# The first two chunks times the first weight pair in float32: a fused attention and MLP kernel on one core

## The chip, the cores and the metric

The kernel runs on one core of a Trainium2 chip. The metric is the device time of one execution in microseconds (us). Engines are called by the profile's names: PE is TensorE (PEld its weight loads), DVE is VectorE, ACT is ScalarE, POOL is GpSimd, and SP is SyncE, which here only starts transfers.

## The reference

A decaying linear attention (4 batches, 8 heads, 768 tokens, 64 per head) is followed by a two-layer perceptron with a leaky ReLU over 3072 tokens, 512 wide, with 2048 hidden units. The inputs of the attention are float32, the weights are float64, and the output is float32.

```python
for b in range(nb):                                   # blocks of 64 tokens
    intra = einsum('bhic,bhjc->bhij', qb, kb) * Dmask # Dmask: lam ** (i - j), lower triangle
    intra = einsum('bhij,bhjd->bhid', intra, vb)
    inter = einsum('bhid,bhde->bhie', qb * lam_pow, kv_state)
    out[:, :, sl] = intra + inter
    kv_state = lam_block * kv_state + einsum('bhsd,bhse->bhde', kb * rev_pow, vb)
x = out.transpose(0, 2, 1, 3).reshape(B * S, H * D)   # 3072 x 512
h = x @ w_in                                          # 512 -> 2048
g = maximum(0.01 * h, h)
y = g @ w_out                                         # 2048 -> 512
```

## The kernel before

**Chunks and groups.** The 3072 tokens are 24 chunks of 128, six per batch. Four chunks make a group of 512 tokens, so there are six groups (0 to 5). The weights w_in are cut into eight pairs of 128 hidden units (0 to 7).

**Attention of a chunk.** `load_kq` and `load_v` fetch keys, queries and values. `transposes` (L391) turns keys and queries on PE, ACT copies them out of PSUM (L402, L403), and keys and queries are scaled by powers of lam (L407 and L411; `KM` and `QS` say up to which chunk DVE may or must do that, after which POOL does). `scores` makes scores and state products in the PSUM tile `psc` (PE, L312; chunks below `GOFIRST` do the scores first), DVE scales the scores (L440) and adds the states (L445, L447), and POOL decays the states (L450). `outputs` makes the chunk's outputs in `po`, in three steps of PE; between the second and third a copy of two columns (L479) reads `po`.

**Three-way split.** PE multiplies in float32r[...]. So tokens and weights are each split into a high part, a low part and a difference: xh, xl, xm (L495 on ACT, L496 and L498 on DVE) and wh, wl, wm (L581 or L579, L584, L590). A product is then three float32r products, high with high, low with low and difference with difference, summed in one PSUM bank; the sum is rescaled by ACT (L646) between the second and the third.

**Weights.** `w_in(p)` (stage "wi") fetches two halves of float64 weights into a raw buffer (issued by ACT, L554), rebuilds float32 values in the tile `w32` (ACT L566, L568, L570; DVE L572, L573), and splits them in `parts`, which ends with `difference`. `w32` holds one pair at a time.

**First layer.** `up(g, p, lo, hi)` multiplies the chunks lo to hi of group g with pair p (L628: each of the three products has four matmuls per half of the pair), applies the leaky ReLU (ACT, L649) into one of two tiles `gs`, and stores the result to the DRAM tile `G` (SP, L652). The PSUM banks b10, b11 and b2 are used in turn. L265 makes transposes of an identity that nobody reads; `busy` puts them where PE is expected to idle. From group 2 on the work is regular. Then the second layer (`down_load`, `down`, L688) reads `G` back and multiplies with the split w_out.

**What sets the order.** A list `seq`, written out by hand for the start, names stages: "a" a whole chunk's attention, "b" the start of the pipelined form, "r" a pipelined round, "wi" a pair of weights, "up" a product. Each stage adds operations with a planned length and their data dependencies to `Plan`; `emit` then places one operation after another on the engine where it can begin first by the planned lengths, ties going to the lower rank (the place in `seq` plus a given addition). This fixes the order of each engine; at run time each engine follows its own order and waits on semaphores. In `up` the planned lengths of the four matmuls of a product are 0.91, 0.7, 0.49 and 0.29 us for 4, 3, 2 and 1 chunks (512, 384, 256 and 128 columns).

Of the kernel before, what the change touches and what calls it, by code (L numbers as in the profile page):

```python
# [8 lines left out]
F32 = mybir.dt.float32  # L9
# [153 lines left out]
def kernel(  # L163
# [21 lines left out]
    NG = NCH // GC  # L185
    T = GC * C
    WARM = 9
    LATER = 2.0
    KT, EARLY = "b11", 0
    QS = 4  # L190
    KM = 2
    NRAW = 3
    TURN = 3
    SLACK, GSLACK = 4.0, 2.0
    EARLY_SLACK = 1.0
    GOFIRST = 3
    SUBL, FIRST = 0.75, -8.0

    DV = 12
# [9 lines left out]
    def sb(shape, name, dt=F32):  # L209
        return pool.tile(shape, dt, name=name, tag=name)  # L210
# [16 lines left out]
    w32f = w32.rearrange("p h n -> p (h n)")  # L227
    tt = [raw[-1][:, i * T:(i + 1) * T] for i in range(2)]
    gs = [sb([P, 2, T], f"gs{i}") for i in range(2)]
    WO = [dram.tile([P, 2 * d_model], F32, name=f"wo{p}", tag=f"wo{p}") for p in range(NP)]  # L230
    G = [[dram.tile([P, 2 * T], F32, name=f"g{g}_{p}", tag=f"g{g}_{p}") for p in range(NP)] for g in range(NG)]

# [222 lines left out]
    def outputs(c, between=lambda: None):  # L455
        b, n, i = of(c)
        tv, qsT = kqv[2][i], qsTs[i]

        def own():
            for y in range(HP):  # L460
                for hi in range(2):
                    for t in range(2):
                        h = 2 * y + hi
                        a, z = place(h)
                        quad(po[:, t, y, :], t, tv[:, h, :], sc[:, a, z, :], hi, start=y == 0)

        def inter(m):
            for y in range(HP):
                t = y % 2 ^ m
                for hi in range(2):  # L470
                    if n or t:
                        a, z = place(2 * y + hi)
                        quad(po[:, t, y, :], a, state[(2 * c + t - 1) % 4][:, z, :], qsT[:, z, tokens(t)], hi)

        needs = [f"qsT{i}", f"st{2 * c % 4}"] + ([f"st{(2 * c - 1) % 4}"] if n else [])
        add("PE", 0.61, own, ["sc", f"v{i}"], ["po"])
        add("PE", 0.24, lambda: inter(0), needs, ["po"])

        add(("DVE", "ACT"), (0.15, 0.25), lambda e: (nc.vector.tensor_copy if e == "DVE" else nc.scalar.copy)(seen_po, po[:, :, 0, 0]),  # L479
            ["po"], ["seen_po"], rank=-3.0)  # L480
        between()
        add("PE", 0.46, lambda: inter(1), needs + ["seen_po"], ["po"])


        g, cc = c // GC, c % GC
        xh, xl, xm = (x[:, :, cc * C:(cc + 1) * C] for x in X[g % 2])
        y = po[:, :, lower, :]

        def tok(z):
            return z.rearrange("p k (t i) -> p t k i", t=2)  # L490

        h, l, m = (f"x{z}{g % 2}{cc}" for z in "hlm")

        def uses():
            add("ACT", 0.6, lambda: nc.scalar.activation(out=tok(xh), in_=y, func=AF.Copy, bias=0.0, scale=NEAR), ["po"], [h])  # L495
            add("DVE", 0.7, lambda: nc.vector.tensor_tensor(tok(xl), y, tok(xh.bitcast(F32)), op=ALU.subtract),  # L496
                ["po", h], [l])
            add("DVE", 0.7, lambda: nc.vector.scalar_tensor_tensor(xm, xl.bitcast(F32), -S, xh.bitcast(F32), op0=ALU.mult, op1=ALU.add),  # L498
                [h, l], [m], rank=LATER if c < GC else 0.0)

        return uses
# [73 lines left out]
    def parts(p, src, keys):  # L575
        wh, wl, wm = W[p]
        def head(e):
            if e == "ACT":
                nc.scalar.activation(out=wh, in_=src, func=AF.Copy, bias=0.0, scale=NEAR / S)  # L579
            else:  # L580
                nc.vector.tensor_scalar(wh, src, NEAR / S, None, op0=ALU.mult)  # L581

        add(("ACT", "DVE"), (1.05, 0.7), head, keys, [f"wh{p}"])
        add("DVE", 1.25, lambda: nc.vector.scalar_tensor_tensor(wl, wh.bitcast(F32), -S, src, op0=ALU.mult, op1=ALU.add),  # L584
            keys + [f"wh{p}"], [f"wl{p}"])
        difference(p)

    def difference(p):
        wh, wl, wm = W[p]
# [3 lines left out]
    def w_in(p):  # L593
        for h in range(2):
            to_float32("wi", p, h, w32[:, h, :], f"w32{h}")
        parts(p, w32f, ["w320", "w321"])

    ATT = ["fk", "fq", "sc"] + [f"{x}{i}" for x in ("k", "q", "v", "kT", "qT", "qsT") for i in range(2)] + [f"st{i}" for i in range(4)]
    NR = 4
# [7 lines left out]
    def w_out_parts(p):  # L607
        j = p % NR
        add("DMA", 1.5, lambda: nc.sync.dma_start(out=graw[j], in_=WO[p]), [f"WO{p}"], [f"gr{j}"], rank=-3.0)
        parts(p, graw[j], [f"gr{j}"])  # L610


    n_t = n_g = 0
    n_b = -EARLY

    def up(g, p, lo=0, hi=GC):


        nonlocal n_g, n_b
        x, w = X[g % 2], W[p]  # L620
        jg, n_g = n_g % 2, n_g + 1
        toks = slice(lo * C, hi * C)
        n = (hi - lo) * C
        us = {4: 0.91, 3: 0.7, 2: 0.49, 1: 0.29}[hi - lo]

        def product(dst, f, z, start=False):
            for kk in range(KO):
                nc.tensor.matmul(dst, lhsT=w[z][:, kk * 2 * P + f * P:kk * 2 * P + (f + 1) * P], rhs=x[z][:, kk, toks],  # L628
                                 start=start and kk == 0, stop=kk == KO - 1, skip_group_check=True)

        def keys(z):
            return [f"w{z}{p}"] + [f"x{z}{g % 2}{cc}" for cc in range(lo, hi)]


        blocks = [[0, 1]] if 2 * n <= T else [[0], [1]]
        y = gs[jg].rearrange("p f t -> p (f t)")[:, :2 * n].rearrange("p (f t) -> p f t", f=2)
        for fs in blocks:
            kb = ("b10", "b2")[n_b % 2] if n_b < 0 else ("b10", "b11", "b2")[n_b % 3]
            n_b += 1
            b = bank[kb][:, :len(fs) * n].rearrange("p (f t) -> p f t", f=len(fs))  # L640
            r = y[:, fs[0]:fs[-1] + 1, :]
            for i, f in enumerate(fs):
                add("PE", us, lambda f=f, d=b[:, i, :], first=i == 0: product(d, f, 0, first), keys("h"), [kb])
                add("PE", us, lambda f=f, d=b[:, i, :]: product(d, f, 1), keys("l"), [kb])
            ns = 0.6 if len(fs) * n == T else 0.4
            add("ACT", ns, lambda b=b: nc.scalar.activation(out=b, in_=b, func=AF.Copy, bias=0.0, scale=S + 1.0), [], [kb], rank=-1.5)  # L646
            for i, f in enumerate(fs):
                add("PE", us, lambda f=f, d=b[:, i, :]: product(d, f, 2), keys("m"), [kb])
            add("ACT", ns, lambda b=b, r=r: nc.scalar.activation(out=r, in_=b, func=AF.Prelu, bias=0.0, scale=1.0 / WS, alpha=0.01),  # L649
                [kb], [f"gs{jg}"], rank=-1.5)  # L650
        move(1.5 * (hi - lo) / GC + 0.1,
            lambda: nc.sync.dma_start(out=G[g][p].rearrange("p (f t) -> p f t", f=2)[:, :, toks], in_=y), [f"gs{jg}"], [f"G{g}{p}"], slack=GSLACK)  # L652

# [22 lines left out]
    def down(g, p):  # L676

        nonlocal n_t
        for tb in range(GC):
# [43 lines left out]

    seq = [("a", 0), ("a", 1), ("a", 2), ("a", 3), ("wi", 1), ("b", 4), ("r", 4), ("up", 0, 1), ("wi", 0), ("r", 5),
# [4 lines left out]
    nxt, n_out, begin = 3 * GC, 0, len(seq)  # L731
    steps = [(g, p) for g in range(2, NG) for p in range(NP)]
    for n, (g, p) in enumerate(steps):
# [12 lines left out]
    for g in range(NG):  # L746
        for p in range(0, NP, 2):
            seq += [("dl", g, p), ("dl", g, p + 1), ("dn", g, p)]

    freed = False  # L750
    for n, x in enumerate(seq):
        plan.rank = float(n)
        steady = begin <= n and x[0] in ("r", "up", "wo")
        if x[0] in "abr":
            {"a": alone, "b": begun, "r": round_of}[x[0]](x[1])
        elif x[0] == "wi":
            w_in(x[1])
        elif x[0] == "up":
            up(*x[1:])
        elif x[0] == "wo":  # L760
            w_out(*x[1:])
        elif x[0] == "wp":
            if not freed:
                add("DVE", 0.0, lambda: None, [], ATT + [f"gr{j}" for j in range(NR)])
                add("ACT", 0.0, lambda: None, [], [f"raw{j}" for j in range(NRAW)] + ["t0", "t1"])
                freed = True
            w_out_parts(x[1])
        elif x[0] == "dl":
            plan.rank = n - 8.0
            down_load(*x[1:])  # L770
        else:
            down(*x[1:])
# [31 lines left out]
```

## Time and profile before

| quantity | value |
|---|---|
| median of 3 runs | 612.86 us (612.7 to 613.33) |
| the profiled execution, its own time | 614.14 us |
| its span, first to last instruction | 612.3 us |
| PE busy | 600.5 us, 98% of the span |
| DVE busy | 312.2 us, 51% |
| ACT busy | 270.9 us, 44% |
| POOL busy | 83.0 us, 14% |
| first float32r product of the first layer | 31.94 us |

A line of instruction groups in the profile gives code line, engine, operation, the tiles written and read, the shape and the count; then the busy time and the mean length of one in ns; then the idle time of the engine ahead of it and what ended that. A timeline line gives start and length in us first. A line of the chain of waits gives the same for the chain that ended last. The recorded length of a matmul is more than the time until the next can start, since matmuls overlap, so costs of PE work are read from the distances between starts. The dummy transposes of L265 count as busy PE.

### The profile page before, as it was taken

The numbers are of one execution on the slowest core, as the hardware profiler recorded it, in microseconds if no ns is written. First come the engines' busy times: TensorE is split into PE (matmuls) and PEld (weight loads), VectorE is DVE, ScalarE is ACT, GpSimd is POOL, SyncE is SP. The second block draws the span as 40 slices with busy tenths as digits, with TensorE's granted clock in tenths as the row PEclk, the third lists the DMA queues.
The fourth block names the chain that finished last, engine by engine and source line by source line (L and its number), as shares of the span: only waits on it lengthen the run. The fifth ranks groups of instructions, "written<-read, shape, count | busy, mean of one in ns | idle before, by whom it ended". The sixth has DMA issues, their size and how long they took to land.

```text
span 612.3 us, 12915 instructions
## 1 busy us (share of the span) xinstructions
PE 600.5 (98%) x5402; PEld 498.1 (81%) x5402; DVE 312.2 (51%) x412; ACT 270.9 (44%) x434; POOL 83.0 (14%) x90
## 2 busy tenths in 40 slices
PE   8899999999999999999999999999999999999997
PEld 6677888888888888888788888888888888888886
DVE  3899981064353344326356845535454554635531
ACT  2778884444465655556577522221222313214111
POOL 1563410053233013103000000000000000000000
PEclk9999999999999999999999999999999999999999
DMA  9999876544889969876776842523433343433201
GB/s 205 219 248 255 237 205 169 152 123 131 192 207 253 234 192 244 219 237 172 287 263 223 286 161 88 187 70 126 149 101 122 120 135 106 138 103 121 86 1 69
DMA packets 141162, 104.66 MB, mean 171 GB/s; under 512 B 117040, under 2 KB 117808, under 8 KB 141104
## 3 DMA queue, kind: packets, MB, share of 16 engines
q1 hardware_dynamic: 136608, 95.44, 53.7%
q10 hardware_dynamic: 4496, 8.39, 4.5%
q8 instruction: 42, 0.69, 0.5%
q14 instruction: 16, 0.13, 0.1%
HBM read 68.16 MB, written 35.65 MB: 170 GB/s over the span
## 4 chain that ended last, share of the span: by engine, by line
PE 93%; DVE 4%; DMA 1%; POOL 1%; issue 0%; SPq 0%; ACT 0%; DVEq 0%; ACTq 0%; POOLq 0%
PE b L628 41%; PE b L688 18%; PE po L688 11%; PE psc L688 11%; PE po L312 4%; PE pt L688 4%; PE psc L312 3%; DVE w L572 1%; DVE w L573 1%; DMA att<-in_v_dram 1%; PE pt L391 1%; DVE wm L590 0%; DVE att L447 0%; DVE wl L584 0%; DVE wh L581 0%
## 5 line engine op out<-in xcount | busy, mean ns | idle before, releaser
L670 ACT ACTIVATE xh<-att 128x1024 fp32r<-128x1024 f32 x48 | 50.9, 1061 | 147.1 <-PE b L688 145.4
L671 DVE SCALAR_TENSOR_TENSOR xl<-att,xh 128x1024 fp32r<-128x1024 f32 x48 | 58.7, 1223 | 99.0 <-ACT xh L670 99.0
L628 PE MATMUL b<-xl,wl 128*128 128x512 f32 (+1 forms) x392 | 102.9, 386 | 0.6 <-DVE wl L584 0.6
L628 PE MATMUL b<-xh,wh 128*128 128x512 f32 (+1 forms) x392 | 102.7, 386 | 0.8 <-ACT xh L495 0.8
L628 PE MATMUL b<-xm,wm 128*128 128x512 f32 (+1 forms) x392 | 103.2, 391 | 0.0
L628 PEld LDWEIGHTS b<-xh,wh 128*128 128x128 f32 x392 | 72.7, 188 | 16.1 <-ACT xh L495 0.9
L628 PEld LDWEIGHTS b<-xl,wl 128*128 128x128 f32 x392 | 72.5, 188 | 15.7 <-DVE wl L584 1.0
L628 PEld LDWEIGHTS b<-xm,wm 128*128 128x128 f32 x392 | 71.3, 188 | 14.6
L649 ACT ACTIVATE gs<-b 128x512 f32<-128x512 f32 x96 | 57.2, 597 | 47.9 <-PE b L628 44.1
L646 ACT ACTIVATE b<-b 128x512 f32<-128x512 f32 x96 | 56.0, 585 | 50.4 <-PE b L628 50.3
L688 PE MATMUL b<-wl,xl 128*128 128x512 f32 x192 | 74.7, 389 | 0.0
L688 PE MATMUL b<-wh,xh 128*128 128x512 f32 x192 | 74.7, 389 | 0.0
L673 DVE SCALAR_TENSOR_TENSOR xm<-xl,xh 128x1024 fp32r<-128x1024 f32 x48 | 58.8, 1226 | 5.1 <-DVE xl L671 0.5
L440 DVE TENSOR_TENSOR att<-psc,att 128x512 f32<-128x512 f32 x24 | 16.5, 689 | 64.6 <-PE psc L312 64.5
L688 PEld LDWEIGHTS b<-wl,xl 128*128 128x128 f32 x192 | 36.1, 188 | 7.5
L688 PEld LDWEIGHTS b<-wh,xh 128*128 128x128 f32 x192 | 36.0, 188 | 7.5
L407 POOL TENSOR_TENSOR att<-att 128x512 f32<-128x512 f32 (+1 forms) x23 | 25.8, 1123 | 100.7 <-PE po L391 55.2
L450 POOL TENSOR_TENSOR att<-att 128x256 f32<-128x256 f32 x40 | 32.8, 820 | 45.7 <-DVE att L447 45.7
L572 DVE TENSOR_SCALAR w<-w 128x512 int32<-128x512 int32 x32 | 18.2, 569 | 39.5 <-ACT w L566 39.5
L688 PE MATMUL po<-wl,xl 128*128 128x512 f32 x96 | 37.4, 390 | 0.0
L688 PE MATMUL psc<-wh,xh 128*128 128x512 f32 x96 | 37.4, 389 | 0.0
L688 PE MATMUL psc<-wm,xm 128*128 128x512 f32 x96 | 37.4, 389 | 0.0
(73 smaller groups left out, 812.1 us busy)
## 6 DMA issues: line engine op xcount, KB each, us to landing
att<-g SPq DMA_DIRECT2D x48, 512.0 KB, 3.3
g<-gs SPq DMA_DIRECT2D x47, 512.0 KB, 3.9
raw<-in_moe_w_in_dram ACTq DMA_DIRECT2D x16, 512.0 KB, 4.9
raw<-in_moe_w_out_dram SPq DMA_DIRECT2D x16, 512.0 KB, 4.6
att<-in_k_dram SPq DMA_DIRECT2D x48, 128.0 KB, 4.6
att<-in_v_dram SPq DMA_DIRECT2D x24, 256.0 KB, 4.4
out_dram<-gs SPq DMA_DIRECT2D x23, 256.0 KB, 2.0
wo<-w SPq DMA_DIRECT2D x8, 512.0 KB, 5.7
```

What stands on the lines that cost most here:

```text
L312: nc.tensor.matmul(dst[HALF[cols]], lhsT=lhsT[HALF[rows]], rhs=rhs[HALF[rows]], start=start, stop=True, skip_group_check=True)
L407: lambda e="POOL": ENG[e].tensor_tensor(kr[nr], kr[nr], _bc(pow_k, 3, D)[nr], op=ALU.mult), ["fk"], [f"k{i}"])
L440: add("DVE", 0.69, lambda: nc.vector.tensor_tensor(sc, psc[:, :, lower, :], decay, op=ALU.mult), ["psc", "fk"], ["sc"])
L450: add("POOL", 0.7, lambda new=new, j=j: nc.gpsimd.tensor_tensor(state[(j + 1) % 4], new, _bc(lam_c, 2, D), op=ALU.mult), [f"st{j % 4}", "f ...
L572: add("DVE", 0.42, lambda: nc.vector.tensor_scalar(d, d, 3, None, op0=ALU.logical_shift_left), [], [key])
L628: nc.tensor.matmul(dst, lhsT=w[z][:, kk * 2 * P + f * P:kk * 2 * P + (f + 1) * P], rhs=x[z][:, kk, toks], start=start and kk == 0, stop=kk ...
L646: add("ACT", ns, lambda b=b: nc.scalar.activation(out=b, in_=b, func=AF.Copy, bias=0.0, scale=S + 1.0), [], [kb], rank=-1.5)
L649: add("ACT", ns, lambda b=b, r=r: nc.scalar.activation(out=r, in_=b, func=AF.Prelu, bias=0.0, scale=1.0 / WS, alpha=0.01), [kb], [f"gs{jg} ...
L670: add("ACT", 1.05, lambda: nc.scalar.activation(out=h, in_=graw[j], func=AF.Copy, bias=0.0, scale=NEAR), reads, wr("h"))
L671: add("DVE", 1.25, lambda: nc.vector.scalar_tensor_tensor(l, graw[j], 1.0, h.bitcast(F32), op0=ALU.mult, op1=ALU.subtract), reads + [f"rh{ ...
L673: add("DVE", 1.25, lambda: nc.vector.scalar_tensor_tensor(m, l.bitcast(F32), -S, h.bitcast(F32), op0=ALU.mult, op1=ALU.add), [f"rh{j}", f" ...
L688: nc.tensor.matmul(acc[tb][z // 2][:, cols], lhsT=ring[j][z][:, f * T + tb * P:f * T + (tb + 1) * P], rhs=W[pp][z][:, f * d_model:(f + 1) ...
```

## The change

For chunks 0 and 1 (`WHOLE = 2`) ACT copies the attention's output whole into a float32 tile `x32` (which lies in the second `gs` tile), and xh, xl and xm are made from there. The product of chunks 0 and 1 with pair 1 is taken directly in float32 from `x32` and `w32` (`product32`), with one application of the leaky ReLU and no rescaling. The rest of group 0 with pair 1 is done chunk by chunk, in 128 columns each. For the pairs in `APART` (1, 2, 6, 4) the difference wm is a stage of its own, "wd", later in the list. The list `seq` is rewritten: the product of group 0 with pair 5 is cut into three chunks and one, that of group 1 with pair 1 into two, one and one, and other stages change places. Some constants change: which bank takes the transposes and how many products alternate between two banks (`KT`, `EARLY`), DVE scales the queries of two chunks instead of four (`QS`), POOL scales all keys (`KM`), and chunk 3 also does its scores first (`GOFIRST`). The operations and their order on each engine follow from `Plan` as before.

```diff
-    LATER = 2.0
-    KT, EARLY = "b11", 0
-    QS = 4
-    KM = 2
+    LATER = 4.0
+    KT, EARLY = "b2", 2
+    QS = 2
+    KM = 0
+    APART = (1, 2, 6, 4)
+    WHOLE = 2
+    SPLIT = 0.0
...
-    GOFIRST = 3
+    GOFIRST = 4
...
+    x32 = gs[1].rearrange("p f t -> p (f t)").rearrange("p (k t) -> p k t", k=KO)
...
+        def whole():
+            s, xs = x32[:, :, cc * C:(cc + 1) * C], f"xs{cc}"
+            add("ACT", 0.6, lambda: nc.scalar.copy(tok(s), y), ["po"], [xs])
+            add(("ACT", "DVE"), (0.6, 0.45), lambda e: nc.scalar.activation(out=xh, in_=s, func=AF.Copy, bias=0.0, scale=NEAR) if e == "ACT"
+                else nc.vector.tensor_scalar(xh, s, NEAR, None, op0=ALU.mult), [xs], [h], rank=SPLIT)
+            add("DVE", 0.7, lambda: nc.vector.tensor_tensor(xl, s, xh.bitcast(F32), op=ALU.subtract), [xs, h], [l], rank=SPLIT)
+            add("DVE", 0.7, lambda: nc.vector.scalar_tensor_tensor(xm, xl.bitcast(F32), -S, xh.bitcast(F32), op0=ALU.mult, op1=ALU.add),
+                [h, l], [m], rank=max(SPLIT, LATER))
...
-        difference(p)
...
         parts(p, w32f, ["w320", "w321"])
+        if p not in APART:
+            difference(p)
...
+        jg, n_g = (0, n_g) if plan.rank <= last_whole else (n_g % 2, n_g + 1)
+        kg = [f"gs{jg}"] + [f"xs{cc}" for cc in range(WHOLE) if jg and g < 2]
...
+        def product32(dst, f, start):
+            for kk in range(KO):
+                nc.tensor.matmul(dst, lhsT=w32f[:, kk * 2 * P + f * P:kk * 2 * P + (f + 1) * P], rhs=x32[:, kk, toks],
+                                 start=start and kk == 0, stop=kk == KO - 1, skip_group_check=True)
...
+            for i, f in enumerate(fs if whole else ()):
+                add("PE", 0.875 * (hi - lo), lambda f=f, d=b[:, i, :], first=i == 0: product32(d, f, first),
+                    ["w320", "w321"] + [f"xs{cc}" for cc in range(lo, hi)], [kb])
...
-    seq = [("a", 0), ("a", 1), ("a", 2), ("a", 3), ("wi", 1), ("b", 4), ("r", 4), ("up", 0, 1), ("wi", 0), ("r", 5),
-           ("wi", 2), ("wi", 3), ("up", 0, 0), ("up", 0, 2), ("r", 6), ("up", 0, 3), ("up", 1, 1, 0, 2), ("wi", 7),
-           ("wi", 6), ("up", 0, 7), ("r", 7), ("wi", 5), ("up", 1, 7), ("wi", 4), ("up", 1, 2), ("up", 0, 6),
-           ("up", 0, 5), ("up", 0, 4), ("up", 1, 0), ("up", 1, 6), ("up", 1, 1, 2, 4), ("r", 8), ("up", 1, 5),
-           ("r", 9), ("r", 10), ("up", 1, 3), ("r", 11), ("up", 1, 4)]
+    seq = [("a", 0), ("a", 1), ("a", 2), ("wi", 1), ("a", 3), ("b", 4), ("whole", 0, 1, 0, 2), ("r", 4), ("wd", 1),
+           ("wi", 0), ("up", 0, 1, 2, 3), ("r", 5), ("up", 0, 1, 3, 4), ("wi", 2), ("wd", 2), ("up", 0, 0), ("wi", 3),
+           ("up", 0, 2), ("up", 0, 3), ("r", 6), ("r", 7), ("wi", 7), ("up", 1, 1, 0, 2), ("wi", 6), ("up", 0, 7),
+           ("wi", 4), ("wi", 5), ("up", 1, 7), ("wd", 6), ("up", 1, 2), ("wd", 4), ("up", 0, 4), ("up", 0, 5, 0, 3),
+           ("up", 0, 5, 3, 4), ("up", 0, 6), ("r", 8), ("r", 9), ("up", 1, 4), ("up", 1, 0), ("up", 1, 1, 2, 3),
+           ("r", 10), ("up", 1, 6), ("r", 11), ("up", 1, 1, 3, 4), ("up", 1, 3), ("up", 1, 5)]
```

More of the change, by code (lines that the diff above doesn't have):

```diff
@@ L492, in outputs @@
         h, l, m = (f"x{z}{g % 2}{cc}" for z in "hlm")
+        def whole():
[6 more added lines that the diff above has]
+                [h, l], [m], rank=max(SPLIT, LATER))
         def uses():
+            if c < WHOLE:
+                whole()
+                return
             add("ACT", 0.6, lambda: nc.scalar.activation(out=tok(xh), in_=y, func=AF.Copy, bias=0.0, scale=NEAR), ["po"], [h])
@@ L610, in w_out_parts, with up @@
         parts(p, graw[j], [f"gr{j}"])
+        difference(p)
     n_t = n_g = 0
     n_b = -EARLY
-    def up(g, p, lo=0, hi=GC):
+    def up(g, p, lo=0, hi=GC, whole=False):
         nonlocal n_g, n_b
         x, w = X[g % 2], W[p]
-        jg, n_g = n_g % 2, n_g + 1
+        jg, n_g = (0, n_g) if plan.rank <= last_whole else (n_g % 2, n_g + 1)
+        kg = [f"gs{jg}"] + [f"xs{cc}" for cc in range(WHOLE) if jg and g < 2]
         toks = slice(lo * C, hi * C)
@@ L641, in up @@
             r = y[:, fs[0]:fs[-1] + 1, :]
-            for i, f in enumerate(fs):
+            ns = 0.6 if len(fs) * n == T else 0.4
+            for i, f in enumerate(fs if whole else ()):
+                add("PE", 0.875 * (hi - lo), lambda f=f, d=b[:, i, :], first=i == 0: product32(d, f, first),
+                    ["w320", "w321"] + [f"xs{cc}" for cc in range(lo, hi)], [kb])
+            for i, f in enumerate(() if whole else fs):
                 add("PE", us, lambda f=f, d=b[:, i, :], first=i == 0: product(d, f, 0, first), keys("h"), [kb])
                 add("PE", us, lambda f=f, d=b[:, i, :]: product(d, f, 1), keys("l"), [kb])
-            ns = 0.6 if len(fs) * n == T else 0.4
-            add("ACT", ns, lambda b=b: nc.scalar.activation(out=b, in_=b, func=AF.Copy, bias=0.0, scale=S + 1.0), [], [kb], rank=-1.5)
-            for i, f in enumerate(fs):
+            if not whole:
+                add("ACT", ns, lambda b=b: nc.scalar.activation(out=b, in_=b, func=AF.Copy, bias=0.0, scale=S + 1.0), [], [kb], rank=-1.5)
+            for i, f in enumerate(() if whole else fs):
                 add("PE", us, lambda f=f, d=b[:, i, :]: product(d, f, 2), keys("m"), [kb])
             add("ACT", ns, lambda b=b, r=r: nc.scalar.activation(out=r, in_=b, func=AF.Prelu, bias=0.0, scale=1.0 / WS, alpha=0.01),
-                [kb], [f"gs{jg}"], rank=-1.5)
+                [kb], kg, rank=-1.5)
         move(1.5 * (hi - lo) / GC + 0.1,
@@ L748 @@
             seq += [("dl", g, p), ("dl", g, p + 1), ("dn", g, p)]
+    last_whole = max((n for n, x in enumerate(seq) if x[0] == "whole"), default=-1)
     freed = False
@@ L757 @@
             w_in(x[1])
+        elif x[0] == "wd":
+            difference(x[1])
         elif x[0] == "up":
             up(*x[1:])
+        elif x[0] == "whole":
+            up(*x[1:], whole=True)
         elif x[0] == "wo":
```

## The prediction

> **What bounds the kernel now.** I read the busy totals first, then the busy time by stretches of 15 us, then the chain of waits up to 60 us, then TensorE's order of work around its last stall.
>
> ```profile
> PE 600.5 (98%) x5402; PEld 498.1 (81%) x5402; DVE 312.2 (51%) x412; ACT 270.9 (44%) x434; POOL 83.0 (14%) x90
> ```
>
> 98% says little about the start, because the dummy transposes of L265 count as busy. The stretches tell stages apart (columns: sum, then busy time of PE, PEld, DVE, ACT, POOL, then clock and DMA):
>
> ```profile
> 30.00:45.00 15.00, 13.72 (x153) 10.90 (x144) 14.21 (x18) 10.87 (x19) 9.42 (x8) 1.00 0.96 244
> 45.00:60.00 15.00, 14.39 (x289) 12.05 (x288) 14.45 (x20) 12.74 (x25) 6.06 (x5) 1.00 0.88 248
> 60.00:75.00 15.00, 15.00 (x218) 13.14 (x220) 13.92 (x20) 12.66 (x23) 6.77 (x6) 1.00 0.82 244
> ```
>
> From 60 us PE is full, and stays so almost to 604 us (0.28 us of gaps in 250 to 300): work added or removed there counts in full. Before that DVE is the fuller engine. The chain of waits names it piece by piece:
>
> ```profile
> 30.12 1.56 DVE wl L584
> 32.02 1.90 DVE wm L590
> 33.92 0.61 DVE xl L496
> ...
> 47.37 1.24 DVE wh L581
> ...
> 49.54 1.15 DVE wl L584
> 50.73 3.02 PE b L628 x12
> ```
>
> So the chain passes from DVE to PE when the low part wl of weight pair 2 is made. TensorE's order of work at that place (start, length):
>
> ```profile
> 49.05 1.07 PE L628 MATMUL b<-xh,wh 128*128 128x512 f32 x4
> 50.73 1.20 PE L628 MATMUL b<-xl,wl 128*128 128x512 f32 x4 [0.61 <-DVE wl L584]
> 51.76 1.07 PE L628 MATMUL b<-xh,wh 128*128 128x512 f32 x4
> 52.67 1.07 PE L628 MATMUL b<-xl,wl 128*128 128x512 f32 x4
> 53.59 0.60 PE L391 MATMUL po<-att 128*128 128x128 f32 x4
> ```
>
> The stall of 0.61 us is the last; at 53.59 the high and low products of group 0 with pair 2 are done, and all that follows is back to back. I use 53.59 as the meeting point: **the change in time is the shift of this point plus the change in PE work behind it.**
>
> **Prices of a matmul.** The kernel before has float32r products with 512 and 256 columns, none with 128. From starts: eight with 512 columns take 40.49 to 42.30, 0.2275 us each; eight with 256 columns take 70.76 to 71.71, 0.1185. The straight line gives 0.173 for 384 and 0.064 for 128. But each product loads its own weights. At the stall nothing hides a load; PEld's and PE's records there, taken singly:
>
> ```profile
> 50.73 0.19 PEld L628 LDWEIGHTS b<-xl,wl 128*128 128x128 f32 x1 [1.04 <-DVE wl L584]
> 50.84 0.19 PEld L628 LDWEIGHTS b<-xl,wl 128*128 128x128 f32 x1
> ```
>
> ```profile
> 50.73 0.50 PE L628 MATMUL b<-xl,wl 128*128 128x512 f32 x1 [0.61 <-DVE wl L584]
> 51.07 0.40 PE L628 MATMUL b<-xl,wl 128*128 128x512 f32 x1
> 51.30 0.39 PE L628 MATMUL b<-xl,wl 128*128 128x512 f32 x1
> ```
>
> The second load starts 0.11 behind the first, and the first product takes 0.34 to the next start where the second takes 0.23: 0.107 to 0.11 is a load that isn't hidden. Loads overlap products (0.1185 per pair at 256 columns), but follow one another at 0.107 at best. So 128 columns cost 0.107 to 0.1185: I take 0.113, nearly what 256 cost. Float32: the 64x64 products of L312 leave two records each (1472 for 736 in the program), four neighbours every 0.058 us, 0.9 ns a column, where float32r's rows differ by 0.109 us over 256 columns, 0.43 ns. So each record of float32 takes twice float32r's time, a 128x128 product of 256 columns is two records like the 0.2275 row, 0.455, and eight of them 3.64 us (3.4 if only the columns counted, 4.5 if both loads of each showed; I take 3.64).
>
> **The Trainium skill.** "TensorE: Matmul & The Clock Gate", section "LDWEIGHTS (loading the stationary operand)", gives columns / 1.2 in ns, 107 for 128; the 0.107 at the stall agrees. "FP8 and Floating Point Precision", section "TensorE Precision Notes", gives float32 four passes; two records of double length agree. "Perfetto Trace Analysis", section "Optimizing Scalar/DVE Operations", says GpSimd and DVE share a port; the shift L572 (0.41 to 1.28 us for one shape) agrees that something slows DVE beside POOL.
>
> **The change part by part.**
>
> *Behind the meeting point.* Group 1 with pair 1: 48 products of 256 columns (5.69 us) become 24 of 256 and 48 of 128, 2.84 + 5.42 = 8.27: +2.58. Group 0 with pair 5: 24 of 512 (5.46) become 24 of 384 (4.15) and 24 of 128 (2.71): +1.40. Together **+3.98** (3.55 at 0.107, 4.38 at 0.1185). Nothing hides it: PE is full. The attention rounds there are only ordered anew.
>
> *Ahead of it, on PE.* Group 0 with pair 1 was 5.46 us from 31.94. It becomes the float32 3.64 and 48 of 128 columns, 5.42: 9.06, or +3.6. In 24.7 to 31.9 PE has some 3.9 us of gaps and dummies, so this mostly fits. My chain, with durations of before: POOL now also scales chunk 0's keys (L407, 1.06) and chunk 2's queries (L411, 1.27), so chunk 2's state products wait for its keys until 22.6 (22.4 was their end); its score scaling ends at 24.2 on DVE (23.2 before); w32 is whole by 25.2 to 25.7. Float32 of the first half 25.8 to 27.6, chunk 3's scores and state to 28.6, second half to 30.4, chunk 3's outputs to 31.2, 12 small products to 32.6, a transpose, the last outputs to 33.4; chunk 3's xh from ACT at 34.2 (31.9 before); 28 more small products from 33.4 on, about 3.2 us, with two transposes and chunk 4's scores: the products with pair 0 start at 39.8 (40.49 before). From there as before, +8.56: pair 2's high products at 48.4. They now come both first (1.82), so wl of pair 2 is wanted at 50.2.
>
> *Ahead of it, on DVE.* Between 15.5 us and that wl, DVE loses two query scalings (1.38), gains wh of pair 1 (1.24, was ACT), the low part and difference of chunk 4 now ahead of wl (1.38), and a copy (0.15): +1.4. It had about 1.9 us of waits. By my chain wl of pair 2 ends at 51.1 (50.68 before). The remaining low products, 1.94 with an uncovered load, end at 53.1: **shift -0.5**, from -2 (DVE's additions all fall into its waits) to +2 (POOL, with 3.6 us more, slows DVE, or the 3.6 us extra on PE hold the attention chain).
>
> *At nothing.* The two ACT copies to x32 (0.6 each) stand against two rescalings left out; ACT is busy 11 to 13 of 15 us, and if they were on the path they would cost 1.2. Of the four postponed differences, those of pairs 2, 6 and 4 still follow their wl directly in DVE's order; only pair 1's moves, behind a score scaling, a state and a difference, and its users stand at 34 us and later. Without that cover, 1.2. Loads for x32 need no transfer; SP gets seven more stores of G in smaller pieces. They are read back from 352 us on, so they cost nothing; but a store queued ahead of a load holds it: chunk 6's values stand behind two such stores that go at about 40.5, as one store did at 41.3. Pair 1's raw weights now rank ahead of chunk 3's loads; ACT issues them between the same copies as before, so I put this at nothing, but a landing 1 us later would hold the float32 products and the shift by as much. The banks given to transposes and products, and chunk 3's scores ahead of its state, only swap work within the same waits of PE. Pair 4 is now split before pair 5: its wh is wanted near 88, and the seventh split of before had its wl at 86.65, so 2 to 3 us of cover remain; if DVE ran later than that, PE would wait.
>
> **Sum.** +3.98 - 0.5 = +3.5. The profiled execution's own 614.14 (span 612.3 and 1.8 around it) becomes 617.6; the median of the runs, 612.86, becomes **616.3**.
>
> **Rivals.**
> 1. *DVE or POOL starves PE more* (chance 0.18): wl of pair 2 at 53, or a wait at pair 4. Speaks for it: DVE 14.5 of 15 us, POOL heavier. Against: DVE's waits shrink too. 618 to 620.
> 2. *Float32r at 128 columns runs at the rate of float32* (0.07): 0.2275 each. Behind the point 72 x 0.1145 = +8.2; ahead 48 x 0.1145 = 5.5 less 0.9 of slack. 629. No row shows 128 columns; nothing in the 256 row hints at it.
> 3. *Faster* (0.07): loads run two at a time, and 128 columns cost the planner's 0.29 / 4 = 0.0725; the part behind costs only 1.07. With wl of pair 2 made 2.4 earlier: 611.5. It decides once the point moves further ahead than the part behind costs; the load spacing of 0.107 speaks against it.
> 4. *No difference* (0.08): shift -3 with my prices, or the cheap price with little shift. 613.
>
> **How the numbers follow.** The forecast has 0.6 and its own range 614.6 to 618. From 613.0 to 620.8 leaves out rival 2, rival 3 and the edges. 0.2%, 1.2 us, is about what can be told from no change: faster 0.08, same 0.09, slower 0.83.
>
> **What would show it.** Right: float32r products of 128 columns 0.107 to 0.119 apart; float32 ones of 256 columns leave 16 records, 0.2275 apart; PE's last stall still at wl of pair 2, near 51 us; no new gap after 60. Wrong: 128 columns at 0.07 or at 0.2; a stall moved elsewhere; pair 0 started before 38 or after 42.

## The result, and the profile after

| | before | after |
|---|---|---|
| median of the runs beside each other | 613.1 us (612.7 to 614.29, 4 runs) | 618.45 us (618.06 to 618.81, 4 runs) |
| profiled execution, its own time | 614.14 us | 618.53 us |
| its span | 612.3 us | 616.7 us |
| end of the high and low products of group 0 with pair 2 (the meeting point) | 53.59 us | 54.14 us |
| from there to the end of the span | 558.71 us | 562.56 us |

The changed kernel is slower: the ratio is 1.008 with a 95% interval of 1.0062 to 1.0097, or 3.8 to 5.9 us. The forecast was 616.3, with a range of 613.0 to 620.8. The part behind the meeting point grew by 3.85 us, where +3.98 was forecast. The meeting point itself moved by +0.55 between these two profiles, where -0.5 was forecast. The profiles thus differ by 4.4 us, the medians by 5.35; the last microsecond is taken up below.

The busy totals of the changed kernel:

```profile
PE 605.2 (98%) x5485; PEld 504.4 (82%) x5485; DVE 312.8 (51%) x410; ACT 272.0 (44%) x440; POOL 87.5 (14%) x93
```

PE is busy 4.7 us longer at the same share of 98%, and so is the span, by 4.4. Again the total says nothing of the place. The stretches of the changed kernel (columns: sum, then busy time of PE, PEld, DVE, ACT, POOL, then clock and DMA):

```profile
30.00:45.00 15.00, 14.75 (x214) 12.97 (x214) 12.32 (x17) 9.97 (x20) 8.42 (x7) 1.00 0.88 224
...
60.00:75.00 15.00, 15.00 (x239) 13.16 (x240) 14.32 (x20) 12.99 (x23) 7.50 (x6) 1.00 0.85 238
```

From 30 to 45 us PE went from 13.72 to 14.75 busy and DVE from 14.21 down to 12.32: the small products fill PE's idle time, as the prediction's "ahead of it, on PE" said. From 60 us PE is full in both kernels. In each of them its waits after 55 us come to a single one of 0.3 us (in total, times, longest; before, then after):

```profile
PE po L312 <- DVE att L479: 0.3, 1, 0.3
PE po L317 <- DVE att L484: 0.3, 1, 0.3
```

The price of 128 columns is read where the last piece of group 0 with pair 5 runs. TensorE's order of work there, in the changed kernel (start, length):

```profile
101.31 0.85 PE L648 MATMUL b<-xl,wl 128*128 128x384 f32 x4
102.00 0.56 PE L648 MATMUL b<-xh,wh 128*128 128x128 f32 x4
102.40 0.61 PE L648 MATMUL b<-xl,wl 128*128 128x128 f32 x4
...
103.29 0.61 PE L648 MATMUL b<-xl,wl 128*128 128x128 f32 x4
```

From 102.40 to 103.29 eight products take 0.89 us, 0.111 each. From 101.31 to 102.00 four of 384 columns take 0.69, 0.173 each, exactly the straight line. So 128 columns cost 94% of what 256 cost (0.1185) and stand at the spacing of weight loads, 0.107 at the stall of before. The cheap price of 0.0725 and the dear one of 0.2275 both fall.

The same place also shows that it is the load that sets this price, and not a slower passage of 128 columns. PE's and PEld's records, taken nearly singly:

```profile
102.00 0.22 PE L648 MATMUL b<-xh,wh 128*128 128x128 f32 x1
102.01 0.19 PEld L648 LDWEIGHTS b<-xh,wh 128*128 128x128 f32 x1
102.06 0.39 PE L648 MATMUL b<-xh,wh 128*128 128x128 f32 x2
102.12 0.19 PEld L648 LDWEIGHTS b<-xh,wh 128*128 128x128 f32 x1
```

The second product of 128 columns starts 0.06 behind the first, which is the straight line's 0.064: the columns themselves can follow one another that fast. The load for the third begins 0.11 behind the load for the second, and from there each product starts 0.06 behind its own load, so the products keep the loads' distance of 0.11.

The chain of waits of the changed kernel, at its start and at its last stall:

```profile
19.10 7.94 DMA att<-in_v_dram
...
27.18 0.34 PE psc L317 x6
27.52 0.96 issue
28.48 0.68 PE psc L317 x26
...
47.10 0.69 DVE w L590
47.79 0.08 DVE att L484
...
47.91 0.46 PE po L317 x16
```

The first part shows what holds the start in this profile. The values of chunk 3 are asked for at 19.10 and 7.94 us pass until they are used; its state products then stop once more, for 0.96, in which the profile shows nothing that PE waits for. Between them and the products with pair 0 the chain runs mostly on PE. The second part shows the last stall, and it isn't where I put it: a copy of two columns (L484, L479 before) lies on DVE behind a step of rebuilding weights (L590). TensorE's order of work at that place:

```profile
47.91 0.46 PE L317 MATMUL po<-att 64*64 64x64 f32 x16 [0.54 <-DVE att L484]
...
52.19 2.11 PE L648 MATMUL b<-xl,wl 128*128 128x512 f32 x8
54.14 0.60 PE L396 MATMUL po<-att 128*128 128x128 f32 x4
```

The low products show no wait at 52.19. But wl of pair 2 runs on DVE from 50.91 to 52.13, so PE comes just as it is ready, and time won at the copy should only be waited for here. The copy4_act run below tries that.

### The profile page after: what moved, and what is told of

Same layout as the page of the kernel before. It is cut to its first block, busy times and chain, and to the rows that moved or that the text cites. A ratio compares the mean times of both kernels' runs of the same rounds, so it can differ in the third digit from the quotient of the medians.

```text
span 616.7 us, 13104 instructions
## 1 busy us (share of the span) xinstructions
PE 605.2 (98%) x5485; PEld 504.4 (82%) x5485; DVE 312.8 (51%) x410; ACT 272.0 (44%) x440; POOL 87.5 (14%) x93
## 4 chain that ended last, share of the span: by engine, by line
PE 94%; DMA 3%; DVE 1%; SPq 0%; issue 0%; ACT 0%; POOL 0%; ACTq 0%; DVEq 0%
PE b L648 43%; PE b L717 18%; PE po L717 11%; PE psc L717 11%; PE po L317 4%; PE pt L717 4%; PE psc L317 3%; DMA att<-in_v_dram 2%; DMA att<-in_k_dram 1%; PE po L396 1%; SPq L342 0%; PE pt L396 0%; DVE w L589 0%; PE b L653 0%; POOL att L455 0%
## 5 line engine op out<-in xcount | busy, mean ns | idle before, releaser
L648 PE MATMUL b<-xl,wl 128*128 128x512 f32 (+3 forms) x416 | 105.5, 377 | 0.0
L648 PE MATMUL b<-xh,wh 128*128 128x512 f32 (+3 forms) x416 | 105.0, 376 | 0.2 <-ACT xh L512 0.2
L648 PE MATMUL b<-xm,wm 128*128 128x512 f32 (+3 forms) x416 | 104.7, 380 | 0.0
L648 PEld LDWEIGHTS b<-xh,wh 128*128 128x128 f32 x416 | 75.3, 188 | 15.0 <-ACT xh L512 0.4
L648 PEld LDWEIGHTS b<-xm,wm 128*128 128x128 f32 x416 | 73.7, 188 | 14.4
L678 ACT ACTIVATE gs<-b 128x512 f32<-128x512 f32 (+2 forms) x99 | 57.6, 583 | 51.8 <-PE b L648 45.0
L675 ACT ACTIVATE b<-b 128x512 f32<-128x512 f32 (+2 forms) x98 | 56.0, 572 | 53.9 <-PE b L648 53.7
L416 POOL TENSOR_TENSOR att<-att 128x512 f32<-128x512 f32 (+1 forms) x22 | 27.6, 1255 | 91.2 <-PE po L317 63.7
L412 POOL TENSOR_TENSOR att<-att 128x512 f32<-128x512 f32 (+1 forms) x24 | 27.9, 1163 | 82.9 <-PE po L396 43.0
L717 PE MATMUL psc<-wh,xh 128*128 128x512 f32 x96 | 37.3, 389 | 0.0
L717 PE MATMUL psc<-wl,xl 128*128 128x512 f32 x96 | 37.3, 389 | 0.0
L717 PE MATMUL psc<-wm,xm 128*128 128x512 f32 x96 | 37.3, 389 | 0.0
L717 PE MATMUL po<-wh,xh 128*128 128x512 f32 x96 | 37.3, 389 | 0.0
```

The source lines that it names most:

```text
L412: lambda e="POOL": ENG[e].tensor_tensor(kr[nr], kr[nr], _bc(pow_k, 3, D)[nr], op=ALU.mult), ["fk"], [f"k{i}"])
L416: add(eng, us, lambda: e.tensor_tensor(o, x, _bc(pow_q, 2, 2)[:, :, m, :], op=ALU.mult), ["fq", dep], [f"qsT{i}"])
L717: nc.tensor.matmul(acc[tb][z // 2][:, cols], lhsT=ring[j][z][:, f * T + tb * P:f * T + (tb + 1) * P], rhs=W[pp][z][:, f * d_model:(f + 1) ...
```

## The experiments

The theory: the loss is the pieces of 128 columns behind the meeting point, at 0.112 each, plus a small shift of that point. The rivals: the cut itself costs (more matmuls, evictions and stores), whatever its width; or the start, with its copy on DVE and its transfers, makes the loss.

**The late cuts in the changed kernel, undone (late_joined, late_joined_again).**

```diff
-           ("wi", 4), ("wi", 5), ("up", 1, 7), ("wd", 6), ("up", 1, 2), ("wd", 4), ("up", 0, 4), ("up", 0, 5, 0, 3),
-           ("up", 0, 5, 3, 4), ("up", 0, 6), ("r", 8), ("r", 9), ("up", 1, 4), ("up", 1, 0), ("up", 1, 1, 2, 3),
-           ("r", 10), ("up", 1, 6), ("r", 11), ("up", 1, 1, 3, 4), ("up", 1, 3), ("up", 1, 5)]
+           ("wi", 4), ("wi", 5), ("up", 1, 7), ("wd", 6), ("up", 1, 2), ("wd", 4), ("up", 0, 4), ("up", 0, 5),
+           ("up", 0, 6), ("r", 8), ("r", 9), ("up", 1, 4), ("up", 1, 0),
+           ("r", 10), ("up", 1, 6), ("r", 11), ("up", 1, 1, 2, 4), ("up", 1, 3), ("up", 1, 5)]
```

> The changed kernel with its late cuts undone: group 0 with pair 5 in one piece of 512 columns, group 1 with pair 1 in two pieces of 256. All before 75 us stays in the same order. Theory (PE is full behind the meeting point and a 128-column product costs 0.113 us): 3.9 us faster than the changed kernel, so within about 1 us of the kernel before; the meeting point stays at 54.1. Rival (the loss comes from the start, or from stores and activations in small pieces that are not on PE): at most 1 us faster than the changed kernel.

Measured: 614.6 us (613.84 to 616.14, 12 runs), ratio 1.0023 (1.0013 to 1.0032). In the profile the meeting point is at 53.62 and the part behind it is 612.3 - 53.62 = 558.68 us, 0.03 from that of before. So the cuts are the whole of the +3.85 behind the point. The point itself was expected to stay at 54.1, as nothing ahead of it was edited, and comes 0.5 earlier; the two profiles of the changed kernel (after_again is below) differ by as much.

A repeat with other runs:

> The changed kernel with its late cuts undone, once more, beside the other three on one chip. Theory (the start of the changed kernel neither gains nor loses): within 1.3 us of the kernel before.

Measured: 615.08 us (614.11 to 615.98, 7 runs), ratio 1.0037 (1.0024 to 1.005); meeting point 53.97, part behind 558.73. The part behind agrees again, the time doesn't: +2.3 us is more than expected. Of the changed kernel's +5.2 to +5.35, the late cuts are 2.9 (617.95 against 615.08, medians) to 3.85; something of 1.2 to 2.3 us stays that is not behind the meeting point.

**The cut of pair 5 alone, in the kernel before (pair5_3_1, pair5_2_2, pair5_1_1_1_1).** One edit in three sizes; the first:

```diff
-           ("up", 0, 5), ("up", 0, 4), ("up", 1, 0), ("up", 1, 6), ("up", 1, 1, 2, 4), ("r", 8), ("up", 1, 5),
+           ("up", 0, 5, 0, 3), ("up", 0, 5, 3, 4), ("up", 0, 4), ("up", 1, 0), ("up", 1, 6), ("up", 1, 1, 2, 4), ("r", 8), ("up", 1, 5),
```

The second has `("up", 0, 5, 0, 2), ("up", 0, 5, 2, 4)` in its place, the third four single chunks.

> The kernel before with only group 0 x pair 5 cut into three chunks and one. Theory (128 columns cost 0.113, 384 cost 0.173): +1.4 us. Rival (cost falls with the columns, 0.064 for 128): +0.2 us.

> The kernel before with group 0 x pair 5 cut into two and two chunks: as many matmuls (48) as in the 3 and 1 cut, but none under 256 columns. Theory (a weight load of 0.107 us hides behind 256 columns and not behind 128): +0.2 us. Rival (what costs is the cut itself: the number of matmuls, activations and stores): the same +1.4 us as the 3 and 1 cut.

> The kernel before with group 0 x pair 5 cut into four single chunks: 96 matmuls of 128 columns. Theory (0.113 each): 10.85 us instead of 5.46, +5.4 us. Rival (0.064 each by the straight line through 512 and 256 columns): +0.7 us. Second rival (float32r of 128 columns at the float32 rate, 0.2275): +16.4 us.

Beside a median of 613.36 us:

| cut of pair 5 | float32r products | time (us) | ratio | from medians | expected |
|---|---|---|---|---|---|
| 3 + 1 | 24 of 384, 24 of 128 | 614.97 (13 runs) | 1.0021 (1.0011 to 1.0031) | +1.6 | +1.4 |
| 2 + 2 | 48 of 256 | 613.31 (14 runs) | 1.0 (0.9991 to 1.0009) | 0 | +0.2 |
| 1 + 1 + 1 + 1 | 96 of 128 | 618.32 (6 runs) | 1.008 (1.0067 to 1.0093) | +5.0 | +5.4 |

The first two have the same number of products, evictions and stores; only the first has pieces of 128 columns. So the cut itself costs nothing that these runs can tell, and the loss comes with the narrow piece. Four single chunks of one pair cost about as much as the whole change. The parts behind the meeting point say the same, 561.2, 559.1 and 564.7 us: less a wait for a load of keys that the first and third profiles have (0.8 and 0.5), they are +1.7, +0.4 and +5.5 on 558.71.

**Where the last microsecond comes from.** Ahead of the meeting point these three kernels have the same order of instructions on every engine as the kernel before. Yet in their profiles the meeting point is at 51.89, 52.32 and 51.69 us, and in that of before at 53.59. The difference arises early. TensorE's work on chunk 0, in the kernel before:

```profile
11.04 1.11 PE L391 MATMUL b<-att 128*128 128x128 f32 x4
...
12.29 1.56 PE L312 MATMUL po<-att 64*64 64x64 f32 x40
13.78 1.07 PE L391 MATMUL pt<-att 128*128 128x128 f32 x4
```

The same in pair5_2_2, and then its last stall and meeting point:

```profile
10.96 1.11 PE L391 MATMUL b<-att 128*128 128x128 f32 x4
...
12.21 1.17 PE L312 MATMUL po<-att 64*64 64x64 f32 x40
13.32 0.66 PE L391 MATMUL pt<-att 128*128 128x128 f32 x4
...
49.46 1.20 PE L628 MATMUL b<-xl,wl 128*128 128x512 f32 x4 [0.61 <-DVE wl L584]
...
52.32 0.60 PE L391 MATMUL po<-att 128*128 128x128 f32 x4
```

The same four transposes take 1.07 us in one execution and 0.66 in the other: PE works at about half its speed until 14.8 us in the profile of before, and until some 12.5 in this one. With the 40 products ahead of them that makes 0.8 us, and the queries of chunk 0 are copied at 14.89 instead of 14.01. That lateness passes down the chain to the stall (50.73 against 49.46), where it has grown to 1.27; 0.34 of the growth is a longer break in chunk 3's state products, near 27 us (0.68 against 0.34). The profile that I predicted from had caught such a start: its execution took 614.14 us where the median beside it is 613.1.

So the shift has to be measured against ordinary executions of before. What the medians leave for it is 5.35 - 3.85 = **+1.5 us**, and with after_again, below, 5.17 - 3.84 = +1.3. These are remainders. Two things were measured beside them. In the profiles, the point lies at 51.69 to 52.32 in the three cut kernels, which have the start of before, and at 53.62 to 54.14 in the four profiles of the changed start (the changed kernel and late_joined, twice each): 1.9 apart on average. Two of the three early ones then lose 0.8 and 0.5 at the wait for keys, so an early point isn't worth all of its lead. And in the times, late_joined, whose start is that of the changed kernel, lost 1.2 and 2.3 with nothing behind the point. Together they put the shift at 1.2 to 2.3 us. That PE's late start is all that lies between +0.55 and +1.5 is not shown: there is one profile of before.

**The changed kernel again (after_again), its copy elsewhere (copy_act), and less to transfer (skip_raw).**

> The changed kernel as it is, beside the other three on one chip. Both theories: 4.5 to 5.3 us slower than the kernel before.

Measured: 617.95 us (617.74 to 618.91, 6 runs) beside 612.78, ratio 1.0083 (1.007 to 1.0096). Meeting point 53.65, part behind 562.55: the late part repeats to 0.01 us. The wait for the copy is there again, 0.53 us.

The two-column copies all put on ACT:

```diff
-        add(("DVE", "ACT"), (0.15, 0.25), lambda e: (nc.vector.tensor_copy if e == "DVE" else nc.scalar.copy)(seen_po, po[:, :, 0, 0]),
+        add("ACT", 0.25, lambda: nc.scalar.copy(seen_po, po[:, :, 0, 0]),
```

> The changed kernel with the two-column copy of the outputs' PSUM tile fixed to ACT (in the changed kernel DVE makes chunk 4's, behind the rebuilding of weights, and PE waits 0.54 us for it at 47.9). Theory: that wait goes, but the low part of pair 2 is ready at about 52.0 either way and takes over: 0.1 to 0.4 us faster than the changed kernel. Rival (the copy's wait is on the path alone): 0.54 us faster or more.

Measured: 620.17 us (619.67 to 620.63, 4 runs), ratio 1.0116 (1.0101 to 1.0132): 2.2 slower than after_again, a miss. The edit did too much. It moved every such copy, and PE now waits for two of the later ones, on ACT: its waits after 55 us rise from 0.3 to 1.1 us, and the part behind the point from 562.55 to 563.85. At the place in question the wait moved to wl of pair 2, 1.03 us, and the point was not earlier, at 54.05 (53.65 in after_again).

The second half of pair 0's raw weights not fetched:

```diff
-        move(1.6, get, after, [f"raw{j}"])
+        move(1.6, (lambda: None) if (kind, p, h) == ("wi", 0, 1) else get, after, [f"raw{j}"])
```

> The changed kernel without the transfer of the second raw half of pair 0's w_in (issued at 19.2 us, 6.4 earlier than in the kernel before, just behind chunk 3's values at 19.1); the rest of the program is the same, that half is rebuilt from the raw data of pair 1. Theory: this transfer delays chunk 3's values, for which PE waits until 28.5; without it they land 1 to 2 us earlier, the products with pair 0 start up to 1.5 earlier than 40.9, and the time falls by 0.5 to 1.5 us, until DVE's making of pair 2's low part stops it. Rival (PE's added products alone hold chunk 3 and 4): the values land earlier, the time stays within 0.3 us.

Measured: 618.1 us (617.22 to 619.07, 6 runs), ratio 1.0084. Chunk 3's scores and state were done at 27.8 instead of 28.6, the products with pair 0 began at 39.71 instead of 40.36, and the meeting point came at 53.01 instead of 53.65. The point comes 0.64 earlier than in after_again, and 0.61 to 1.13 earlier than in all four profiles of the changed start, which differ by 0.5 among themselves. So this transfer does seem to hold the start, by about that much in one profile. In the time nothing of it is seen (+0.15 by medians, inside both intervals), as the rival said; in the profile 0.4 us of it is lost near 240 us. The place is shown, a gain is not.

**Only chunk 4's copy on ACT, the late cuts joined (copy4_act), and the weight's low part first (wl_first).** These are edits of late_joined, so that nothing else moves:

```diff
-        add(("DVE", "ACT"), (0.15, 0.25), lambda e: (nc.vector.tensor_copy if e == "DVE" else nc.scalar.copy)(seen_po, po[:, :, 0, 0]),
+        add(*((("ACT",), (0.25,)) if c == 4 else (("DVE", "ACT"), (0.15, 0.25))), lambda e="ACT": (nc.vector.tensor_copy if e == "DVE" else nc.scalar.copy)(seen_po, po[:, :, 0, 0]),
```

> The same (late cuts undone), and chunk 4's two-column copy alone moved to ACT; every other instruction keeps its place. Theory (PE's wait of 0.5 us for the copy is covered by DVE: the low part of pair 2 is ready at 51.6 and takes over): PE's stall moves to that low part and is 0.4 to 0.6 us there; the time stays within 0.3 us. Rival (the copy's wait is on the path): 0.5 us faster.

Measured: 614.92 us (614.27 to 615.2, 7 runs), ratio 1.003 (1.0019 to 1.004); 0.16 below late_joined_again. TensorE's order of work at the stall, in copy4_act:

```profile
46.85 2.11 PE L648 MATMUL b<-xm,wm 128*128 128x512 f32 x8
...
51.81 2.12 PE L648 MATMUL b<-xl,wl 128*128 128x512 f32 x8 [1.03 <-DVE wl L601]
53.77 0.60 PE L396 MATMUL po<-att 128*128 128x128 f32 x4
```

The wait for the copy is gone, the products with xm start about 1 us earlier than in late_joined, and all of that is waited for at wl, longer than the 0.4 to 0.6 expected. So at the copy only the name of the stall was new: DVE's making of wl is what sets the point, as in the kernel before.

The edit after it is copy4_act with the low part of chunk 4's tokens ranked behind wl of pair 2:

```diff
-                ["po", h], [l])
+                ["po", h], [l], rank=8.0 if c == 4 else 0.0)
```

> The same with the copy on ACT, and chunk 4's low part and difference (1.4 us of DVE) ranked behind pair 2's low part. Theory (DVE sets the meeting point): the low part of pair 2 is ready at about 50.2 instead of 51.6, the products of group 0 with pair 2 end 0.5 to 0.8 us earlier, and the time falls by as much if nothing behind it comes late. Rival (something else is as late): 0.2 us or less.

Measured: 615.04 us (614.57 to 616.47, 6 runs), ratio 1.0038: no gain, as the rival said of the time. But its profile caught a late start of PE: the scores of chunk 1 were made at 15.66 where copy4_act has 13.34, chunk 3 was done 1.1 us later (29.50 against 28.40) and pair 0 began at 41.28 instead of 40.17. PE then waited 0.61 us at 51.62, for wl again, and the point came at 54.48. DVE's order did what was meant, but its inputs came late; PE's order changed as well, so this doesn't tell what that step is worth.

**No float32 (no_f32_joined), and no 128 columns at all (joined_all).** The first is late_joined with chunks 0 and 1 times pair 1 as three float32r products of 256 columns:

```diff
-    WHOLE = 2
+    WHOLE = 0
...
-    seq = [("a", 0), ("a", 1), ("a", 2), ("wi", 1), ("a", 3), ("b", 4), ("whole", 0, 1, 0, 2), ("r", 4), ("wd", 1),
+    seq = [("a", 0), ("a", 1), ("a", 2), ("wi", 1), ("a", 3), ("b", 4), ("wd", 1), ("up", 0, 1, 0, 2), ("r", 4),
```

> The same late part as late_joined, but chunks 0 and 1 with pair 1 as three float32r products of 256 columns, made from split tokens and weights; no float32 product is left. PE has 0.8 us less to do ahead of the meeting point. Theory (float32 pays because it needs no split weights and so fills PE's idle time): the low products wait for pair 1's low part at about 28.5 and stand ahead of chunk 3's scores, so chunk 3 comes 1 to 2.5 us later, and the time rises by as much less what PE saves, 0.5 to 2 us. Rival (filling doesn't matter, DVE sets the meeting point): within 0.4 us of late_joined.

Measured: 619.55 us (615.49 to 620.53, 6 runs), ratio 1.0092 (1.0065 to 1.0118), 4.5 slower than late_joined_again. The sign is as expected, the size isn't. One line of its stretches shows why it can't be taken as the worth of float32:

```profile
40.00:43.00 3.00, 3.00 (x12) 2.48 (x11) 1.38 (x2) 0.94 (x2) 0.00 (x0) 0.50 0.25 71
```

In this profile the granted clock is 0.52 from 37 to 40 us and 0.50 from 40 to 43, where late_joined_again has 1.00. Four of the six executions have a mean clock of 0.993 or 0.994 and took 619.4 to 620.5; the two with 0.999 and 0.996 took 615.49 and 616.1, that is 0.4 and 1.0 above late_joined_again. Two executions are too few: what the float32 itself gains stays open.

The second joins both the late cuts and chunks 2 and 3 in the start, with the copies on ACT:

```diff
-           ("wi", 0), ("up", 0, 1, 2, 3), ("r", 5), ("up", 0, 1, 3, 4), ("wi", 2), ("wd", 2), ("up", 0, 0), ("wi", 3),
+           ("wi", 0), ("r", 5), ("up", 0, 1, 2, 4), ("wi", 2), ("wd", 2), ("up", 0, 0), ("wi", 3),
```

> The changed kernel with no product of 128 columns at all: late cuts undone, chunks 2 and 3 of group 0 with pair 1 in one piece of 256 columns, the copy on ACT; float32 for chunks 0 and 1 stays. Theory: 3.98 us saved behind the meeting point; ahead of it PE has 2.6 less, so pair 0 starts at about 39 and the meeting point is set by pair 2's low part at 51 to 52: 0.5 to 1 us earlier than 54.1, so the time is between 0.5 us faster than the kernel before and 0.5 slower. Rival (float32 itself costs at the start): 1 us or more slower than the kernel before.

Measured: 618.45 us (617.26 to 620.54, 6 runs), ratio 1.0094 (1.0076 to 1.0112), a miss. The waits of PE after 55 us in joined_all (total, times, longest):

```profile
PE po L317 <- ACT att L484: 1.1, 2, 0.8
PE b L648 <- ACT gs L678: 1.0, 1, 1.0
PE b L648 <- ACT xh L512: 0.8, 1, 0.8
PE b L648 <- ACT b L675: 0.7, 1, 0.7
```

These are 3.6 us where the kernel before has 0.3, so most of what the joined pieces gave back went into new waits for ACT. Some 2.4 of the 5.7 us on the kernel before are not in them, and the expectation's rival, that float32 itself costs at the start, is not ruled out. In the start PE waited 1.03 us for chunk 3's xh and 1.06 for its xl; in the changed kernel chunk 2's small products lie there, and the wait for xh is 0.25. So the small pieces ahead of the point seem to fill a gap; what joining them alone would cost isn't separated from the copies here.

None of these kernels is faster than the kernel before; the best is equal to it (pair5_2_2).

## Why the prediction was right, and where its sizes were off

**Behind the meeting point: right.** The sum of +3.98, from 72 products of 128 columns at 0.113 and the others by the straight line, measured +3.85 in two profiles of the changed kernel, and 0 with the cuts undone. "Nothing hides it" was right too: no new wait of PE after 60 us. The step that decided it was to price 128 columns by the weight load seen at a stall and not by the columns; only the first product of a narrow piece, behind a wide one, costs the columns' 0.06.

**The Trainium skill** page named there for the load, "TensorE: Matmul & The Clock Gate", section "LDWEIGHTS (loading the stationary operand)", gives columns / 1.2 in ns, which is 107 for 128 columns; loads in the changed kernel follow one another at 0.109 to 0.112 us, which agrees, as a floor.

**Float32: nearly right.** TensorE's order in the changed kernel shows the first half:

```profile
24.13 1.99 PE L653 MATMUL b<-gs,w 128*128 128x256 f32 x8
26.06 0.69 PE L317 MATMUL psc<-att 64*64 64x64 f32 x32
```

Sixteen records in all, as said, eight in each half; a half takes 1.93 us, 0.241 a record, where I had 0.2275 and 1.82. The first half starts 1.7 us earlier than my chain had it (25.8) and gains nothing by that, since the second half comes behind chunk 3's state products, which end at 29.1 where I had 28.6. (The low end given for the eight products, 3.4, should have been 3.5 by the 0.43 ns a column beside it.)

**The shift: the term that was mis-sized.** The prediction put it at -0.5, with -2 to +2 as its ends; it is +0.55 against the profile of before, and about +1.5 against ordinary executions. So the forecast time was 2.15 too low, and the whole range held because it left that much room for this term. Three steps of it were off.
- "wl of pair 2 ends at 51.1" measured 52.13. DVE's work was counted nearly right (from chunk 0's query scaling to that wl its recorded lengths sum to 37.3 us, 35.5 before: +1.8 for the +1.4 forecast), but all of it came later: chunk 3's xh at 35.07 instead of 34.2, pair 0 at 40.85 instead of 39.8. The delay arises at chunk 3's scores and state, to which I gave 1.0 us: they take 3.0, from 26.06 to 29.08, with two breaks of 1.4 us in all, one of them for the values. The transfer that skip_raw leaves out, pair 0's second half, issued 6.4 us earlier than before, is not in my account at all; what I put "at nothing" was pair 1's weights, which no run tried. In after_again, where PE started late as in the profile that I worked from, there is no such break: chunk 3's state ended at 28.58 and pair 0 began at 40.36, nearer to my chain.
- "A copy (0.15)" counted the copy's length and not its place in DVE's order, behind the rebuilding of weights; PE waited 0.54 us for it. By copy4_act that was no loss of its own.
- "The median of the runs, 612.86, becomes 616.3" carried a shift measured on a late execution over to the median. The profiled execution of before, with PE's late start, stands 1.0 to 1.3 us above the medians of its runs, and the changed kernel's profiled execution stands at its own (618.53 against 618.45). That is the size of the 1.0 us between +0.55 and +1.5.

**The rivals.** Rival 1 (PE starved, 618 to 620) gave a time near the measured one, and part of its mechanism: the start is held longer than I forecast. But it wanted wl of pair 2 at 53 or a wait at pair 4, and neither came (52.13, and no wait); 3.85 us of the loss is the late part. Rivals 2 and 3 fall with the price of 0.112, rival 4 with the result. The own range of 614.6 to 618 was missed by 0.45 us, the whole range held.

## What to carry to other kernels

Price a small matmul by its weight load: at 128 columns the load was the cost here, so halving a piece from 256 columns to 128 nearly doubled the work (0.111 us a product against 0.1185), while cutting 512 into 256 was free within what the times can tell. Find the point from which the engine is back to back; cuts that let work start earlier can pay only ahead of it, and each piece below the load's price behind it counts in full. Before adding a shift to a median, see whether the profiled execution is itself an ordinary one: compare its time with the median, and the length of one early operation with the same shape later.

## What the runs showed of the hardware that I had not expected

- In the first 15 us of a program TensorE's speed differs between executions of the same order of instructions: four 128x128 transposes took 1.11 and 1.07 us in before, 1.11 and then 0.66 in pair5_2_2, and 0.66 from 9.1 us on in the changed kernel's profile, with 1.11 again in after_again. The clock column shows 1.00 for the late stretch of before all the same, and 0.53 for that of after_again.
- In before this lateness reached the meeting point (1.3 to 1.9 us of difference). In the changed kernel it did so less: the slow start of after_again scaled chunk 1's scores 1.4 us later (15.96 against 14.54) and had its meeting point 0.5 earlier (53.65 against 54.14), while in wl_first a start later by 2.3 us left pair 0 1.1 later than in copy4_act. I read that as the changed start having a break for transfers that a late PE partly covers: the values of chunk 3 hold PE in the profile of the changed kernel, and not in that of after_again. No run shows it directly.
